# Storing the last block's results in token order over the partitions, by two engines

## The chip, the cores and the metric

One NeuronCore of a Trainium2 chip runs the whole kernel. The metric is the device time of one execution in microseconds, the median over several runs. A profile of one execution stands beside it; its span runs from the first to the last instruction.

## The reference

A causal depthwise convolution over seven tokens, whose weights are the softmax of a small table (one row per head of 24 channels), is followed by a two-layer network with an exact Gelu:

```python
w = softmax(weight, axis=-1)                      # [8 heads, 7 taps]
x_pad = zeros of 6 tokens before each sequence, then x    # x: [8, 4096, 192]
out = einsum('hk,bskhg->bshg', w, windows_of_7(x_pad))    # depthwise convolution
x = out.reshape(32768, 192)
h = x @ w_in                                      # w_in: [192, 2048]
g = 0.5 * h * (1.0 + erf(h / sqrt(2)))
return g @ w_out                                  # w_out: [2048, 192], f32 result
```

## The kernel before, in words

The 32768 tokens are taken as two halves (`HALF` = 16384) that are worked on together. Each half is cut into `NB` = 33 blocks: six of 256 tokens and 27 of 512 (`WS`). Block n covers tokens `OFF[n]` onwards of both halves. There is no planner; every engine has its own program, written out by hand, and semaphores tie them together.

For each block, DMAs on SP load the input (`load`, L258), VectorE transposes it in squares of 32x32 (L478) and convolves it by multiply-and-add (L501, L508) into `xc`; the first two blocks are convolved by TensorE instead. TensorE then computes the first layer one slice of 128 hidden features at a time (`mm1`, L683): both halves of the tokens stand in one of two PSUM buffers `hp[u % 2]`, 2 x 512 columns. ScalarE applies Gelu to each slice (L612) and writes bf16 into `gT[n % 2]`, in which a slice takes 1024 columns. `mm1` of slice u waits for the Gelu of slice u - 2 through `S_GELU`, since it reuses its buffer. Between the slices of block n, TensorE does the second layer of block n - 1.

Because of the 32x32 transposes and of the way in which the input is loaded, column 32b + r of a block stands for token 16r + b of it. For the Gelu of the last block (n = 32) the slice is read as two halves of four runs of 128 columns and written in runs of 128.

The second layer has two forms. Blocks 6 to 31 (`M0` to `M1` - 1) use `mm2_t` (L747), whose result comes out with channels on the partitions, and VectorE transposes it into `osb` (`evac_t`, L247). The last block, and the first six, use `mm2` (L714): the activations are the weights that are loaded into TensorE, 128 tokens at a time, and the result has tokens on the partitions and the 192 channels in the free dimension. A group g of the last block is 128 tokens of the first half of all tokens and 128 of the second, in two PSUM banks of `ob`; there are four groups. Nothing but this is left for TensorE once the last slice's `mm1` and block 31's `mm2_t` are done. Its order is: groups 0 and 1 in two phases of 16 steps each, the phases alternating between the groups, then groups 2 and 3 in the same manner. Group 0's first eight steps wait for half of the Gelus of the block, its next eight for all of them. Group 1 waits for block 31's last VectorE transpose, and groups 2 and 3 wait in `wait_banks` until the banks that they reuse have been copied.

Each group's result leaves PSUM by `evac` (L227 on ScalarE in the first six blocks, L229 on VectorE in the last): one copy of 2 x 192 columns into `osb`. Partition 32q + k of it holds the token 16k + 4g + q of the block, one of each half. `store_group` (L272) therefore stores it in four DMAs, one for each q: 32 partitions by two halves by 768 bytes, in rows 16 tokens apart. For the last block, q = 0 and 1 go out on SP's queue, 2 and 3 on ScalarE's. `OUTS` counts what each parity of blocks adds to `S_OUT`, and at the end SP waits for all of it.

Of the kernel before, what the change touches and what calls it, by code (L numbers as in the profile page):

```python
# [6 lines left out]
AF = mybir.ActivationFunctionType  # L7
# [4 lines left out]
def bass_lightweight_conv__then__act_gelu_exact_kernel(  # L12
# [10 lines left out]
    F2, C = moe_w_out.shape  # L23
# [4 lines left out]
    HALF = NTOK // 2  # L28
    TB = 512
# [7 lines left out]
    NB = len(WS)  # L37
    OFF = [sum(WS[:n]) for n in range(NB)]
    assert sum(WS) == HALF
    NP = D // 64  # L40
    NF = F // 128
# [17 lines left out]
    outt = out.tensor  # L59
# [5 lines left out]
    NG = [w // 128 for w in WS]  # L65
# [5 lines left out]
    PHC, MMC, EVC = [0], [0], [0]  # L71
# [11 lines left out]
    PLAIN = [NCH[n] > 1 or n == NB - 1 for n in range(NB)]  # L83
    assert all(WS[n] == TB for n in range(M0, NB))

    OUTS = []
    for n in range(NB):
        OUTS.append((64 * NG[n] if PLAIN[n] else 64) + (OUTS[n - 2] if n >= 2 else 0))

    es = ExitStack()  # L90

    def sbt(name, shape, dt):
        return es.enter_context(nc.sbuf_tensor(name, shape, dt))

    def pst(name, shape):
        return es.enter_context(nc.psum_tensor(name, shape, F32))

    def sem(name):
        return es.enter_context(nc.semaphore(name))

    def ap(t, off, pat):
        return bass.AP(t, off, pat)

    with es:
# [20 lines left out]
        gT = [sbt("gT%d" % i, [128, NF * 2 * TB], BF16) for i in range(2)]  # L125
        osb = [sbt("osb%d" % i, [128, 8 * C], F32) for i in range(2)]
        hp = [pst("hp%d" % i, [128, 2 * TB]) for i in range(2)]
# [10 lines left out]
        S_OUT = [sem("S_OUT%d" % i) for i in range(2)]  # L138
# [15 lines left out]
        S_GELU = sem("S_GELU")  # L154
        S_MM2 = sem("S_MM2")
        S_PH = sem("S_PH")
        S_EV = sem("S_EV")
        S_EVA = sem("S_EVA")

        block = es.enter_context(nc.Block())  # L160

        def bank(b, r=slice(0, 128), w=512):
            return ob[r, 512 * (b % 4) : 512 * (b % 4) + w]
# [30 lines left out]
        def banks(m, g):  # L194

            if m < M0:
                return (0, 1) if (G0[m] + g) % 2 == 0 else (2, 3)
            r = NP * (M1 - 1 - M0)
            e = (G0[m] - G0[M1] + g) % 2
            return sorted((b % 4 for b in ((r + 3, r), (r + 1, r + 2))[e]))  # L200

        def wait_ev(e, m, g):

            if m < NA:
                e.wait_ge(S_EVA, G0[m] + g + 1)
            else:
                e.wait_ge(S_EV, EVC[m] + g + 1)

        def wait_banks(t, m, g):

            k = G0[m] + g
            if m < M0:
                if k >= 2:
                    t.wait_ge(S_EVA, k - 1)
            else:
                e = k - G0[M1]
                t.wait_ge(S_EV, EVC[M1] + (-2 if e == 0 else e - 1))

        def evac(e, m, g):
            e.wait_ge(S_MM2, MMC[m] + g + 1)  # L220
            if m >= 2 and g == 0:
                e.wait_ge(S_OUT[m % 2], OUTS[m - 2])
            b0, b1 = banks(m, g)
            dst = ap(osb[m % 2], g * C, [[8 * C, 128], [4 * C, 2], [1, C]])
            src = ap(ob, 512 * b0, [[2048, 128], [512 * (b1 - b0), 2], [1, C]])
            if m < NA:
                e.activation(out=dst, in_=src, func=AF.Copy).then_inc(S_EVA)  # L227
            else:
                e.tensor_copy(dst, src).then_inc(S_EV)  # L229

# [34 lines left out]
        def store_group(e, m, g, qs=(0, 1, 2, 3)):  # L267

            mb = WS[m] // 32
            wait_ev(e, m, g)  # L270
            for q in qs:
                e.dma_start(  # L272
                    ap(
                        outt,
                        (OFF[m] + 4 * g + q) * C,
                        [[mb * C, 32], [HALF * C, 2], [1, C]],
                    ),
                    ap(
                        osb[m % 2],
                        32 * q * 8 * C + g * C,  # L280
                        [[8 * C, 32], [4 * C, 2], [1, C]],
                    ),
                ).then_inc(S_OUT[m % 2], 16)
# [109 lines left out]
        def _(v):  # L393
# [142 lines left out]
            side = [((2, (0, 3, 5)[p]), conv_out, 1, p) for p in range(NP)]  # L536
# [2 lines left out]
                    side.append((at, evac_t, v, n, j))  # L539
            for n in range(M1, NB):  # L540
                for g in range(NG[n]):
                    side.append(((n + 3, g), evac, v, n, g))
            side.sort(key=lambda q: q[0])
            for b in range(2, NB):
                if b in PC:
# [9 lines left out]
        @block.scalar  # L555
        def _(a):
            a.wait_ge(S_WARM, 1)
            a.activation(out=hot[:, 0:1], in_=warm[0:1, 0:1], func=AF.Exp).then_inc(S_ACTP)
            load(a, 0, (2, 3))
            a.wait_ge(S_ACTP, 1)  # L560
            a.wait_ge(S_PRO, 1)
            a.activation(
                out=wex[:, :],
                in_=wsb[:, :],
                func=AF.Exp,
                bias=wmx[:, 0:1],
                accum_out=wsm[:, 0:1],
            ).then_inc(S_ACTP)
            a.activation(out=hot[:, 1:2], in_=warm[0:1, 0:1], func=AF.Gelu).then_inc(S_HOT)
            for p in range(NP):  # L570
                a.wait_ge(S_TR, p + 1)
                a.activation(  # L572
                    out=ap(xTb[0], p * XB + HL, [[NP * XB, 128], [1, WS[0]]]),
                    in_=ap(xT[0], p * XW + HL, [[NP * XW, 128], [1, WS[0]]]),
                    func=AF.Copy,
                ).then_inc(S_CAST[0])
            for p in range(NP):
                a.wait_ge(S_PC, p + 1)
                a.activation(  # L579
                    out=xc[0][:, p * TB : p * TB + WS[0]],  # L580
                    in_=bank(CONVB[0][p], w=WS[0]),
                    func=AF.Copy,
                ).then_inc(S_PCE)

            due = {(1, 6): [(0, 0)]}
            for m in range(NA):
                if m >= 1:
                    due[m + 1, NSL[m + 1] // 2] = [(m, 0)]
                due[m + 2, 0] = [(m, 1)]
            for n in range(NB):  # L590
                w = WS[n]
                for i in range(NSL[n]):
                    u = SL0[n] + i
                    c = NCH[n]
                    for k in due.get((n, i), []):
                        evac(a, *k)
                    a.wait_ge(S_MM1, u + 1)
                    if i == 0 and n >= 2:
                        a.wait_ge(S_MM2, MMC[n - 1])
                    if M0 <= n < M1:  # L600

                        src = [[2 * TB, 128], [1, 2 * TB]]
                        dst = [[NF * 2 * TB, 128], [1, 2 * TB]]
                    elif not PLAIN[n]:

                        src = [[2 * TB, 128], [w // 4, 8], [32, w // 128], [1, 32]]
                        dst = [[NF * 2 * TB, 128], [32, 8], [256, w // 128], [1, 32]]
                    else:

                        src = [[2 * TB, 128], [TB, 2], [128, 4], [1, 128]]  # L610
                        dst = [[NF * 2 * TB, 128], [128, 2], [256, 4], [1, 128]]
                    a.activation(  # L612
                        out=ap(gT[n % 2], i * c * 2 * w, dst),
                        in_=ap(hp[u % 2], 0, src),
                        func=AF.Gelu,
                    ).then_inc(S_GELU)

            for g in range(NG[NB - 1]):
                store_group(a, NB - 1, g, (2, 3))

        @block.tensor
        def _(t):
# [70 lines left out]
            def mm2(m, g, ph, i):  # L693
# [4 lines left out]
                if i == 0:  # L698
                    if ph == 0:
                        wait_banks(t, m, g)  # L700
                    else:
                        t.wait_ge(S_PH, PHC[m] + g + 1)
# [25 lines left out]
            def mm2_t(m, ps, i):  # L728

                w = WS[m]  # L730
                if i == 0:
                    if ps < 2:
                        if m == M0:
                            t.wait_ge(S_EVA, G0[M0] - 1 + ps)
                        else:
# [57 lines left out]
        @block.sync  # L793
        def _(sp):
            sp.dma_start(wsb[:, :], ap(wt, 0, [[KS, H], [1, KS]])).then_inc(S_WSB, 16)  # L795
            load(sp, 0, (0, 1))
            sp.wait_ge(S_WIN[0], 32)
            load(sp, 1, (0, 1))
            sp.wait_ge(S_XG[3], 64)
            for n in range(1, NB):  # L800
                if n + 3 < NB:
                    load(sp, n + 3)
                store(sp, n - 1)
            for g in range(NG[NB - 1]):
                store_group(sp, NB - 1, g, (0, 1))
            for s in range(2):
                sp.wait_ge(S_OUT[s], OUTS[NB - 1 if (NB - 1) % 2 == s else NB - 2])

# [27 lines left out]
```

## Time and profile before

| what | value |
|---|---|
| median of 3 runs | 686.33 us (686.32 to 689.21) |
| the profiled execution's own time | 686.27 us |
| its span | 684.5 us |
| TensorE busy | 677.3 us (99% of the span), clock 1.000 |
| VectorE busy | 580.5 us (85%) |
| ScalarE busy | 532.6 us (78%) |
| Gelu instructions (L612) | 512 of 128x1024, 1024 ns each |
| copies of the last block (L229) | 4 of 128x384, 557 ns each |
| stores of the last block (L272) | 16 DMAs of 48 KB, 8 on SP and 8 on ScalarE's queue |
| last TensorE work ends | 681.05 us |

A line of a group gives the source line, the engine and operation, the tile written and the tile read, the shape and the count; then its busy time and the mean length of one instruction; then the idle time of the engine just before them and what ended it. In the timeline a line gives start, length, engine and line, and the idle time before it in brackets; several instructions in a row are merged. PEld is the loading of weights into TensorE, which runs beside its matmuls.

### The profile page before, as it was taken

To read this page: it belongs to the slowest core of one execution; us is meant where nothing else is said; L and a number is where in the kernel's file an instruction comes from. 1 tells how busy PE (TensorE), PEld (TensorE's weight loads), DVE (VectorE), ACT (ScalarE), POOL (GpSimd) and SP (SyncE) were. 2 spreads that over 40 slices of the span, in tenths; PEclk is the share of its full clock that TensorE was granted. 3 is DMA by queue.
4 is the path that set the end of the run, shared out by engine and by line. 5 is a ranking of instruction groups with operands and counts; after the bars stand their busy time and mean duration, and the time that the engine had idled before them with its cause. 6 is when DMAs were issued, how large, how long until landed. Compare 5 with 4: busy or idle time off the path is not lost.

```text
span 684.5 us, 27314 instructions
## 1 busy us (share of the span) xinstructions
PE 677.3 (99%) x12548; PEld 409.0 (60%) x12548; DVE 580.5 (85%) x914; ACT 532.6 (78%) x536; POOL 46.0 (7%) x97
## 2 busy tenths in 40 slices
PE   8999999999999999999999999999999999999997
PEld 4899655555555555555555555555555555555556
DVE  7999999888899888898888898888898888998702
ACT  6788987877787777787877878777778777877771
POOL 8110000000000000000000000000000000000000
PEclk9999999999999999999999999999999999999999
DMA  8544531344432344422444422444322444221224
GB/s 135 95 107 99 117 61 32 64 94 95 94 67 50 76 94 95 93 52 55 85 94 95 88 51 53 95 94 95 72 54 66 95 94 95 61 53 31 48 49 94
DMA packets 133234, 53.66 MB, mean 78 GB/s; under 512 B 127552, under 2 KB 132960, under 8 KB 133120
## 3 DMA queue, kind: packets, MB, share of 16 engines
q1 hardware_dynamic: 128144, 48.78, 33.3%
q0 software_dynamic: 3792, 2.56, 2.4%
q8 instruction: 98, 1.61, 1.0%
q10 hardware_dynamic: 1184, 0.59, 0.3%
q14 instruction: 16, 0.13, 0.1%
HBM read 28.31 MB, written 25.17 MB: 78 GB/s over the span
## 4 chain that ended last, share of the span: by engine, by line
PE 96%; ACT 2%; DMA 1%; issue 0%; DVE 0%; SPq 0%
PE hp L683 47%; PE ob L747 42%; PE ob L714 6%; ACT gT L612 2%; PE ob L640 1%; DMA xin<-in_x_dram 1%; ACT osb L227 0%; DVE osb L247 0%; SPq L258 0%; DVE osb L229 0%; DVE xT L478 0%; ACT xTb L572 0%; SPq L795 0%; ACT xc L579 0%
## 5 line engine op out<-in xcount | busy, mean ns | idle before, releaser
L612 ACT ACTIVATE gT<-hp 128x1024 bf16<-128x1024 f32 x512 | 523.4, 1024 | 132.7 <-PE hp L683 129.6
L683 PE MATMUL hp<-xc,win 64*64 64x512 bf16 (+2 forms) x6048 | 418.5, 366 | 1.1 <-ACT gT L612 0.7
L747 PE MATMUL ob<-gT,wout 64*64 64x512 bf16 x5376 | 366.3, 376 | 0.0
L508 DVE SCALAR_TENSOR_TENSOR acc<-xT,wcol,acc 128x512 f32<-128x512 f32 (+1 forms) x495 | 314.0, 697 | 0.0
L683 PEld LDWEIGHTS hp<-xc,win 64*64 64x64 bf16 (+1 forms) x6048 | 187.7, 106 | 135.6 <-ACT gT L612 2.1
L747 PEld LDWEIGHTS ob<-gT,wout 64*64 64x64 bf16 x5376 | 172.1, 118 | 123.0
L247 DVE STREAM_TRANSPOSE osb<-ob 128x512 f32<-128x512 f32 x84 | 73.7, 880 | 86.8 <-PE ob L747 86.8
L478 DVE STREAM_TRANSPOSE xT<-xin 128x512 f32<-128x512 f32 (+1 forms) x105 | 78.5, 799 | 0.2 <-DMA xin<-in_x_dram 0.2
L508 DVE SCALAR_TENSOR_TENSOR xc<-xT,wcol,acc 128x512 bf16<-128x512 f32 (+1 forms) x99 | 65.1, 711 | 0.0
L374 POOL COPY xT<-xT 128x558 f32<-128x558 f32 x33 | 21.6, 654 | 578.6 <-DVE xT L478 578.6
L501 DVE TENSOR_SCALAR acc<-xT,wcol 128x512 f32<-128x512 f32 (+1 forms) x99 | 56.1, 618 | 1.1
L714 PE MATMUL ob<-wout,gT 64*128 64x192 bf16 x1024 | 52.2, 243 | 0.3
L714 PEld LDWEIGHTS ob<-wout,gT 64*128 64x128 bf16 x1024 | 43.5, 94 | 6.5 <-PE ob L714 0.6
L357 POOL COPY xT<-xT 128x18 f32<-128x18 f32 x30 | 11.6, 387 | 1.4 <-DVE xc L461 1.4
L229 DVE COPY osb<-ob 128x384 f32<-128x384 f32 x4 | 2.2, 557 | 7.8 <-PE ob L714 7.8
L625 PE MATMUL hp<-warm 128*128 128x512 bf16 x16 | 5.7, 533 | 1.3 <-DVE warm L394 1.3
L640 PE MATMUL ob<-xTb,dg 64*64 64x256 bf16 x84 | 5.3, 271 | 1.1 <-ACT xTb L572 1.1
L227 ACT ACTIVATE osb<-ob 128x384 f32<-128x384 f32 x12 | 5.8, 486 | 0.0
L258 POOL DMA_DIRECT2D xin<-in_x_dram x10 | 5.8, 588 | 0.0
L640 PEld LDWEIGHTS ob<-xTb,dg 64*64 64x64 bf16 x84 | 4.3, 106 | 2.2 <-ACT xTb L572 1.6
L625 PEld LDWEIGHTS hp<-warm 128*128 128x128 bf16 x16 | 2.0, 129 | 4.5 <-issue 2.7
L324 POOL DMA_DIRECT2D win<-in_moe_w_in_dram x6 | 3.9, 651 | 0.0
(32 smaller groups left out, 21.7 us busy)
## 6 DMA issues: line engine op xcount, KB each, us to landing
xin<-in_x_dram SPq DMA_DIRECT2D x116, 192.0 KB, 4.4
out_dram<-osb SPq DMA_DIRECT2D x112, 192.0 KB, 3.6
out_dram<-osb SPq DMA_DIRECT2D x56, 48.0 KB, 1.7
xin<-in_x_dram SPq DMA_DIRECT2D x12, 96.0 KB, 2.7
xin<-in_x_dram POOLq DMA_DIRECT2D x10, 96.0 KB, 2.7
wout<-in_moe_w_out_dram POOLq DMA_DIRECT2D x1, 768.0 KB, 8.6
win<-in_moe_w_in_dram POOLq DMA_DIRECT2D x4, 96.0 KB, 4.2
win<-in_moe_w_in_dram POOLq DMA_DIRECT2D x2, 192.0 KB, 5.3
```

What stands on the lines that cost most here:

```text
L247: v.transpose(ap(osb[m % 2], j, [[8 * C, 128], [C // 2, TB // 32], [NP, 32]]), bank(ring(m, j)),).then_inc(S_EV)
L357: g.tensor_copy(dst, ap(xT[(n - 1) % 2], WS[n - 1] + 31, [[NP * XW, 128], [XW, NP], [32, HB]],),).then_inc(S_HALO)
L374: g.tensor_copy(ap(t, 1, [[NP * tw, 128], [tw, NP], [32, HB], [1, 31]]), ap(t, WS[n], [[NP * tw, 128], [tw, NP], [32, HB], [1, 31]]),).the ...
L478: v.transpose(ap(xT[n % 2], p * XW + HL, [[NP * XW, 128], [1, w]]), ap(xin[n % NX], p, [[TB // 32 * DQ, 128], [DQ, w // 32], [NP, 32]],),) ...
L501: ins = v.tensor_scalar(a, src, wk, None, ALU.mult)
L508: ins = v.scalar_tensor_tensor(dst, src, wk, a, op0=ALU.mult, op1=ALU.add)
L612: a.activation(out=ap(gT[n % 2], i * c * 2 * w, dst), in_=ap(hp[u % 2], 0, src), func=AF.Gelu,).then_inc(S_GELU)
L625: t.matmul(hp[1][:, 0:512], warm[:, 0:128], warm[:, :])
L640: ins = t.matmul(bank(CONVB[n][p], r, w), dg[r, d0 : d0 + 64], xTb[PC[n]][r, x0 : x0 + w], start=(k == KS - 1), stop=(k == 0), tile_positi ...
L683: ins = t.matmul(hp[u % 2][fo : fo + fw, o : o + w], win[r, f1 : f1 + fw], xc[n % 2][r, p * TB : p * TB + w], start=(p == 0), stop=(p == N ...
L714: ins = t.matmul(bank(bb[sub], w=C), gT[m % 2][r, c0 : c0 + 128], wout[r, CH[i] * C : (CH[i] + 1) * C], start=(ph == 0 and i == 0), stop=( ...
L747: ins = t.matmul(bank(ring(m, j), slice(64 * h, 64 * h + 64), w), ap(wout, 64 * hf * NF * C + CH[i] * C + j, [[NF * C, 64], [NP, 64]],), g ...
```

## The change

Only the last block is touched. Its Gelu becomes two instructions of 512 elements for each slice, one for each half of the tokens, and writes the results into `gT` in token order: of the 128 columns of a group, column 16k + b gets the token of that number. TensorE, which loads these columns as weights, then puts the group's tokens on the partitions in order. A group's two halves leave PSUM separately: VectorE copies the first half's 192 columns (`evac_half` with h = 0, counted in `S_EV`), ScalarE the second half's (h = 1, counted in the new semaphore `S_EVB`). `store_half` stores each half as one DMA of 128 partitions by 768 bytes, which is one contiguous stretch of the output: the first half on SP's queue, the second on ScalarE's. `wait_banks` waits for both copies for groups 2 and 3. `OUTS` counts eight DMAs for the last block, where it counted sixteen.

```diff
-        OUTS.append((64 * NG[n] if PLAIN[n] else 64) + (OUTS[n - 2] if n >= 2 else 0))
+        k = 32 * NG[n] if n == NB - 1 else 64 * NG[n] if PLAIN[n] else 64
+        OUTS.append(k + (OUTS[n - 2] if n >= 2 else 0))
...
+        S_EVB = sem("S_EVB")
...
                 e = k - G0[M1]
                 t.wait_ge(S_EV, EVC[M1] + (-2 if e == 0 else e - 1))
+                if e >= 2:
+                    t.wait_ge(S_EVB, e - 1)
...
+        def evac_half(e, g, h):
+
+            m = NB - 1
+            e.wait_ge(S_MM2, MMC[m] + g + 1)
+            if g == 0:
+                e.wait_ge(S_OUT[m % 2], OUTS[m - 2])
+            dst = osb[m % 2][:, (4 * h + g) * C : (4 * h + g + 1) * C]
+            src = bank(banks(m, g)[h], w=C)
+            if h == 0:
+                e.tensor_copy(dst, src).then_inc(S_EV)
+            else:
+                e.activation(out=dst, in_=src, func=AF.Copy).then_inc(S_EVB)
+
+        def store_half(e, g, h):
+
+            m = NB - 1
+            if h == 0:
+                wait_ev(e, m, g)
+            else:
+                e.wait_ge(S_EVB, g + 1)
+            e.dma_start(
+                ap(outt, (h * HALF + OFF[m] + 128 * g) * C, [[C, 128], [1, C]]),
+                osb[m % 2][:, (4 * h + g) * C : (4 * h + g + 1) * C],
+            ).then_inc(S_OUT[m % 2], 16)
...
-                    side.append(((n + 3, g), evac, v, n, g))
+                    side.append(((n + 3, g), evac_half, v, g, 0))
...
+                    if n == NB - 1:
+
+                        for h in range(2):
+                            ins = a.activation(
+                                out=ap(
+                                    gT[n % 2],
+                                    i * 2 * w + 128 * h,
+                                    [[NF * 2 * TB, 128], [1, 16], [256, 4], [16, 8]],
+                                ),
+                                in_=ap(
+                                    hp[u % 2],
+                                    TB * h,
+                                    [[2 * TB, 128], [32, 16], [8, 4], [1, 8]],
+                                ),
+                                func=AF.Gelu,
+                            )
+                        ins.then_inc(S_GELU)
+                        continue
...
             for g in range(NG[NB - 1]):
-                store_group(a, NB - 1, g, (2, 3))
+                evac_half(a, g, 1)
+                store_half(a, g, 1)
...
             for g in range(NG[NB - 1]):
-                store_group(sp, NB - 1, g, (0, 1))
+                store_half(sp, g, 0)
```

## The prediction

> **What bounds the kernel now.** I read the chain of waits first, then the cost groups, then the last 40 us in order of time, because only the last block (n = 32) is edited. The page's chain and groups:
>
> ```profile
> PE 96%; ACT 2%; DMA 1%; issue 0%; DVE 0%; SPq 0%
> ...
> L612 ACT ACTIVATE gT<-hp 128x1024 bf16<-128x1024 f32 x512 | 523.4, 1024 | 132.7 <-PE hp L683 129.6
> L683 PE MATMUL hp<-xc,win 64*64 64x512 bf16 (+2 forms) x6048 | 418.5, 366 | 1.1 <-ACT gT L612 0.7
> ...
> L229 DVE COPY osb<-ob 128x384 f32<-128x384 f32 x4 | 2.2, 557 | 7.8 <-PE ob L714 7.8
> ...
> L227 ACT ACTIVATE osb<-ob 128x384 f32<-128x384 f32 x12 | 5.8, 486 | 0.0
> ```
>
> TensorE is the chain. ScalarE's Gelu (L612) waits for TensorE 129.6 us in all and TensorE almost never for it. How thin that cover is, the timeline of the last block shows (start, length, what ran, idle before):
>
> ```profile
> 649.05 0.82 PE L683 MATMUL hp<-xc,win 64*64 64x512 bf16 x12
> ...
> 664.60 1.02 ACT L612 ACTIVATE gT<-hp 128x1024 bf16<-128x1024 f32 x1 [0.27 <-PE hp L683]
> 665.89 1.02 ACT L612 ACTIVATE gT<-hp 128x1024 bf16<-128x1024 f32 x1 [0.27 <-PE hp L683]
> 667.19 1.02 ACT L612 ACTIVATE gT<-hp 128x1024 bf16<-128x1024 f32 x1 [0.27 <-PE hp L683]
> 668.48 2.10 ACT L612 ACTIVATE gT<-hp 128x1024 bf16<-128x1024 f32 x2 [0.27 <-PE hp L683]
> ```
>
> Starts are 1.295 us apart (1.51 three times, 1.08 at the end): TensorE's pace of a slice. ScalarE works 1.02 of it and idles 0.27. The stretch from 649.9 to 670.6 us holds the 16 Gelus of the last block, the first at 649.92, straight after L683 ended. Then the end, in the timeline and in the waits from 668 us on:
>
> ```profile
> 669.99 1.57 DVE L247 STREAM_TRANSPOSE osb<-ob 128x512 f32<-128x512 f32 x2 [6.45 <-PE ob L747]
> 670.64 0.61 PEld L714 LDWEIGHTS ob<-wout,gT 64*128 64x128 bf16 x16 [0.16 <-ACT gT L612]
> 671.62 9.19 PEld L714 LDWEIGHTS ob<-wout,gT 64*128 64x128 bf16 x224 [0.37 <-DVE osb L247]
> ...
> 675.07 7.46 ACTq L272 DMA_DIRECT2D out_dram<-osb  x8
> 675.16 7.29 SPq L272 DMA_DIRECT2D out_dram<-osb  x8
> ...
> 681.08 0.56 DVE L229 COPY osb<-ob 128x384 f32<-128x384 f32 x1 [0.76 <-PE ob L714]
> ```
> ```profile
> PEld ob L714 <- DVE osb L247: 0.4, 1, 0.4
> PEld ob L714 <- ACT gT L612: 0.2, 1, 0.2
> ```
>
> TensorE takes the second half of group 0's first phase at 670.64, released by the last Gelu (ended 670.58), then waits 0.37 us for block 31's transposes, then runs 9.43 us to 681.05. One VectorE copy and the last stores follow, to 684.5: 3.45 us behind TensorE.
>
> [...] The trace gives the same slope, (1024 - 384)/(1024 - 256) = 0.833 ns from L612 and L579 (128x256, 384 ns), but a fixed 171 ns; five Gelus in a row took 4.92 us, so the overlap is (5 x 1.024 - 4.92)/4 = 50 ns. [...]
>
> **The change part by part.**
>
> *Gelu split and permuted.* Sixteen instructions of 1024 elements become 32 of 512. They still read PSUM in order, but write each 2-byte result 32 bytes from the one before (step 16 bf16); before, runs of 128 were contiguous. If the stride is free, one takes 171 + 512 x 0.833 = 598 ns, and in a row 548 ns: a pair 1.10 us, inside 1.295, so hidden by TensorE's slice. The last pair then ends about 0.15 us later than 670.58, and the 0.37 us wait for L247 takes that.
> If the stride costs, ScalarE becomes the bound, as hp has two buffers and L683 of slice u+2 waits for Gelu u. With a pair of P us back to back, the last Gelu ends at 649.92 + 16P + 0.05, TensorE resumes 0.06 later, and the delay against 671.62 - 0.61 = 671.01 is **16P - 20.98 us**: nothing up to P = 1.31.
> The price is unknown, so I bound it. Below: 0.833 ns an element, P = 1.10; a gain is excluded, as the count of elements and the fixed parts don't fall. Above: three cycles an element, P = 2 x (0.121 + 512 x 0.0025) = 2.80, delay 23.8. For nothing: VectorE's transpose L247 writes 4-byte results 12 bytes apart at 880 ns, and L478, which writes contiguously, takes 862. [...] For a price: POOL's memset of 128x18 with 128-byte steps takes 133 ns against 99 for 128x1, 2.0 ns an element, and in bf16 with 64-byte steps 179 against 102, 4.5 ns (POOL spans are rough). I take **two cycles**[...]: 121 + 512 x 1.667 = 974 ns, P = 1.95, delay 16 x 1.95 - 20.98 = **+10.2 us**. The transposes are not late next: they follow block 31's last L747, which is released by the Gelu two slices earlier, at about 678.4, and end by 680.1, before TensorE resumes at 681.3.
>
> *Evacuation.* Four VectorE copies of 384 (557 ns) become four of 192 plus four ScalarE copies of 192. VectorE: 557 - 192 x 1.04 = 357 ns (its conv row rises 255 ns for 256 elements; bounds 279, half, to 557). ScalarE: 171 + 160 = 331 ns, side by side with VectorE. Only group 3 is on the path: -0.20 us; the others hide under L714. ScalarE is free there, its Gelus done.
>
> *Stores.* Sixteen DMAs of 48 KB become eight of 96 KB: one each on SP and ACT per group. An issue took a median of 432 ns on SP and 452 on ACT, and the second of a queue started some 0.35 us after the first; that goes. Data per group is the same. Landing: 48 KB took 1.6 us at the fastest and 2.0 in the median, 192 KB 3.9; I take 2.0 for 96 KB (bounds 1.6 and 3.0). After: copies end 681.44, issued 681.47, landed 683.45, where SP's last wait now ends at 684.1: **-0.65 us** with the 0.20 (range -1.0 to +0.4).
>
> *Queues and waits.* ScalarE's copy of group g+1 stands behind its DMA issue of group g. Groups 2 and 3 finish 1.32 us apart; 0.33 + 0.05 + 0.45 fits, and even the longest ACT issue, 0.79, gives 1.17. TensorE's added wait on S_EVB for groups 2 and 3 asks for copies that have 1.32 us of cover, a phase of another group: group 0's banks are copied while group 1's second phase runs, group 1's while group 2's first phase runs; behind it stand L714's weight loads, all waiting together. The S_OUT wait asks for stores of block 30, long landed. I cost these at nothing; the covers gone, 0.1 us each. SP and ACT each have one issue fewer per group; POOL and the input loads are untouched (last load issued at 598 us).
>
> *Sum.* +10.2 - 0.65 = +9.6 us on the profiled execution's 686.27 (span 684.5 and 1.8 around it), which stands 0.06 under the median 686.33: **695.9 us**.
>
> **The rivals.**
> 1. *The stride is free.* For: [...]the rows here show no penalty for 12 bytes. [...] Then only the end moves: 686.33 - 0.65 = 685.7 us, not slower. It decides at P = 1.31, that is (1.31/2 - 0.121)/512 = 1.04 ns an element.
> 2. *A partial price,* 1.25 ns an element: P = 1.52, delay 3.4, net +2.7: 689.1 us.
> 3. *Three cycles:* +23.8 - 0.65: 709.5 us. Only the rough bf16 POOL row speaks for it.
> 4. *The larger DMA takes back what the shorter queue gives:* 3.0 us to landing with a free stride, end at 684.5 against 684.1: 686.7 us. Against: the same bytes go to the same queues.
> 5. *The change doesn't do what it says,* the ACT store lagging behind SP's: at most a second issue, 0.45 us: 686.1.
>
> **How the numbers follow.** A measurement of this kernel can tell about 0.5% (3.4 us) from no change. Two cycles, or near it: 0.56; three: 0.06; partial: 0.06; free, with 4 and 5: 0.32. Of the partial case most is within 0.5%, and 0.02 is kept for a gain over 3.4 us, for which the 3.45 us tail leaves hardly room. Faster 0.02, same 0.36, slower 0.62. The likeliest case's own range: 1.8 to 2.2 cycles, P from 1.78 to 2.12, gives +6.8 to +12.3 net: 693 to 698.6 us. The whole range reaches down to the free case: 685.4 to 698.6; three cycles are left out.
>
> **What would show it.** Gelu instructions of about 1.02 us for 512 elements, back to back with no idle from 650 us on; L683 in the last block waiting for ScalarE; TensorE's last resume near 681 us. If they last 0.60 us with idle left between pairs, the stride is free and my forecast is wrong. For the end: copies of 0.36 and 0.33 us, one issue per queue and group, under 3 us from TensorE's end to the span's.

## The result and the profile after

The changed kernel took **736.88 us** (median of 4 runs, 735.48 to 738.75) against 686.33 us before: a ratio of 1.0728, 95% interval 1.069 to 1.0767, so it is slower by 7.3%. The direction and the mechanism were forecast, the size was not: 695.9 us, with a range that ended at 698.6. The profiled execution took 737.45 us, with a span of 735.1 us.

The page of the changed kernel, first the chain by engine, then the groups that answer to those shown of before:

```profile
PE 87%; ACT 11%; DMA 1%; issue 0%; SPq 0%; DVE 0%
...
L731 PE MATMUL hp<-xc,win 64*64 64x512 bf16 (+2 forms) x6048 | 423.7, 370 | 31.2 <-ACT gT L644 30.1
...
L644 ACT ACTIVATE gT<-hp 128x512 bf16<-128x512 f32 x32 | 69.7, 2681 | 0.1
...
L244 DVE COPY osb<-ob 128x192 f32<-128x192 f32 x4 | 1.4, 358 | 16.0 <-PE ob L762 16.0
...
L246 ACT ACTIVATE osb<-ob 128x192 f32<-128x192 f32 x4 | 1.3, 331 | 11.5 <-PE ob L762 11.5
```

ScalarE's share of the chain went from 2% to 11%. The 32 Gelus of the last block (L644) occupy 69.7 us without idle time; before, the 16 of that block took 16.4 us. One lasts 2681 ns from its start to its end, but neighbours overlap: 32 of them fit in 69.67 us, so the mean distance from start to start is (69.67 - 2.68)/31 = 2.16 us. TensorE's first layer, which before waited for Gelu 0.7 us in all, now waits 30.1 us.

The two copies at the end last 358 and 331 ns, as forecast (357 and 331). With the 557 ns of before, VectorE's shows (557 - 358)/192 = 1.04 ns an element, the slope that the forecast had used.

The timeline of the last block and the end (start, length, idle before):

```profile
650.13 69.67 ACT L644 ACTIVATE gT<-hp 128x512 bf16<-128x512 f32 x32
...
719.85 7.32 PE L762 MATMUL ob<-wout,gT 64*128 64x192 bf16 x118 [5.13 <-ACT gT L644]
725.65 0.33 ACT L246 ACTIVATE osb<-ob 128x192 f32<-128x192 f32 x1 [5.85 <-PE ob L762]
...
732.25 0.33 ACT L246 ACTIVATE osb<-ob 128x192 f32<-128x192 f32 x1 [0.99 <-PE ob L762]
```

The last Gelu ends at 719.80, and TensorE, which had waited 5.13 us for it, resumes at 719.85. Stretches of that time show a second loss. The columns are stretch, its length, then busy time and count for TensorE, weight loads, VectorE, ScalarE and GpSimd, then the granted TensorE clock, the DMA share and GB/s. The changed kernel, then the kernel before:

```profile
714.80:717.70 2.90, 0.00 (x0) 0.00 (x0) 0.38 (x1) 2.90 (x3) 0.00 (x0) 1.00 0.38 74
717.80:719.80 2.00, 0.00 (x0) 0.00 (x0) 0.00 (x0) 2.00 (x1) 0.00 (x0) 0.50 0.92 205
719.80:722.00 2.20, 2.15 (x28) 2.06 (x30) 0.00 (x0) 0.00 (x0) 0.00 (x0) 0.50 0.32 73
722.00:725.70 3.70, 3.70 (x64) 3.59 (x62) 0.05 (x1) 0.05 (x1) 0.00 (x0) 0.65 0.00 0
725.70:732.30 6.60, 6.51 (x158) 6.28 (x154) 1.07 (x4) 0.99 (x4) 0.00 (x0) 1.00 0.22 68
```
```profile
671.00:674.50 3.50, 3.35 (x82) 3.13 (x78) 0.59 (x2) 0.00 (x0) 0.00 (x0) 1.00 0.43 84
674.50:681.10 6.60, 6.54 (x160) 6.31 (x154) 1.67 (x4) 0.00 (x0) 0.00 (x0) 1.00 0.61 139
```

From resuming to the end of group 0 TensorE took 725.62 - 719.85 = 5.77 us; before, the same work without the waits took 674.45 - 671.01 = 3.44. (671.01 is where the work would have begun without the wait for the transposes, as in the prediction; 725.62 and 674.45 are just before the first copies start.) The granted clock had fallen to 0.50 during the wait, and over 722.00 to 725.70 it was 0.65 on average. The other three groups took 6.60 us in both. The spans therefore add up: the block began 0.21 us later, TensorE's resumption was delayed by a further 719.85 - 671.22 = 48.63, the lower clock added 2.33, and the end shrank from 3.45 to 735.1 - 732.22 = 2.88. The sum is 0.21 + 48.63 + 2.33 - 0.57 = 50.6 us, which is 735.1 - 684.5.

### The profile page after: what moved, and what is told of

Read it like the earlier page. It is cut to its first block, busy times and chain, and to the rows that moved or that the text cites. A ratio compares the mean times of both kernels' runs of the same rounds, so it can differ in the third digit from the quotient of the medians.

```text
span 735.1 us, 27329 instructions
## 1 busy us (share of the span) xinstructions
PE 692.6 (94%) x12548; PEld 412.1 (56%) x12548; DVE 579.5 (79%) x914; ACT 586.7 (80%) x556; POOL 45.8 (6%) x97
## 4 chain that ended last, share of the span: by engine, by line
PE 87%; ACT 11%; DMA 1%; issue 0%; SPq 0%; DVE 0%
PE hp L731 43%; PE ob L795 38%; ACT gT L644 9%; PE ob L762 6%; ACT gT L659 2%; DMA xin<-in_x_dram 1%; PE ob L688 1%; ACT osb L231 0%; SPq L287 0%; DVE xT L507 0%; ACT xTb L601 0%; SPq L843 0%; ACT xc L608 0%; DVE osb L244 0%
## 5 line engine op out<-in xcount | busy, mean ns | idle before, releaser
L659 ACT ACTIVATE gT<-hp 128x1024 bf16<-128x1024 f32 x496 | 506.5, 1023 | 128.9 <-PE hp L731 125.8
L731 PE MATMUL hp<-xc,win 64*64 64x512 bf16 (+2 forms) x6048 | 423.7, 370 | 31.2 <-ACT gT L644 30.1
L795 PE MATMUL ob<-gT,wout 64*64 64x512 bf16 x5376 | 372.4, 381 | 0.0
L644 ACT ACTIVATE gT<-hp 128x512 bf16<-128x512 f32 x32 | 69.7, 2681 | 0.1
L762 PE MATMUL ob<-wout,gT 64*128 64x192 bf16 x1024 | 54.8, 251 | 5.3 <-ACT gT L644 5.1
L762 PEld LDWEIGHTS ob<-wout,gT 64*128 64x128 bf16 x1024 | 46.1, 98 | 11.9 <-ACT gT L644 5.4
```

What stands on the lines that cost most here:

```text
L644: ins = a.activation(out=ap(gT[n % 2], i * 2 * w + 128 * h, [[NF * 2 * TB, 128], [1, 16], [256, 4], [16, 8]],), in_=ap(hp[u % 2], TB * h, ...
L659: a.activation(out=ap(gT[n % 2], i * c * 2 * w, dst), in_=ap(hp[u % 2], 0, src), func=AF.Gelu,).then_inc(S_GELU)
L731: ins = t.matmul(hp[u % 2][fo : fo + fw, o : o + w], win[r, f1 : f1 + fw], xc[n % 2][r, p * TB : p * TB + w], start=(p == 0), stop=(p == N ...
L762: ins = t.matmul(bank(bb[sub], w=C), gT[m % 2][r, c0 : c0 + 128], wout[r, CH[i] * C : (CH[i] + 1) * C], start=(ph == 0 and i == 0), stop=( ...
L795: ins = t.matmul(bank(ring(m, j), slice(64 * h, 64 * h + 64), w), ap(wout, 64 * hf * NF * C + CH[i] * C + j, [[NF * C, 64], [NP, 64]],), g ...
```

## Experiments

Ratios compare each kernel with runs of the kernel before on the same chip. Those had a median of 686.44 us beside experiments 1 to 4, 686.45 beside 5, 6, keep_busy and moving_strided, and 687.39 beside keep_busy_end, conv_order and 9.

**1. The Gelu alone (gelu_only).** The kernel before, with this in its Gelu loop:

```diff
+                    if n == NB - 1:
+                        for h in range(2):
+                            ins = a.activation(out=ap(gT[n % 2], i * 2 * w + 128 * h,
+                                    [[NF * 2 * TB, 128], [1, 16], [256, 4], [16, 8]]),
+                                in_=ap(hp[u % 2], TB * h, [[2 * TB, 128], [32, 16], [8, 4], [1, 8]]),
+                                func=AF.Gelu)
+                        ins.then_inc(S_GELU)
+                        continue
```

> Only the change's two Gelu instructions for each slice; copies and stores of the last block as before (the rows of its result then go to other places, so the output's last block is in another order). Theory (the scattered Gelu is all of the loss): 736.88 + 0.6 = about 737.5 us, 32 Gelus at 2.18 us apart, the granted clock again below 1 in the last block. Rival (the new copies, stores or waits cost some of it): clearly under 736.

It took 736.97 us, ratio 1.0736 (1.0716 to 1.0755), with TensorE's first layer waiting 31.3 us for Gelu:

```profile
L701 PE MATMUL hp<-xc,win 64*64 64x512 bf16 (+2 forms) x6048 | 423.0, 369 | 32.4 <-ACT gT L615 31.3
```

The loss lies in the Gelu; the new copies, stores and waits cost none of it that can be seen. With two runs the 0.5 us of the end can't be told.

**2. The end alone (tail_only).** The changed kernel without the lines above.

> The changed kernel with the Gelu of before (one instruction, contiguous runs); each half of a group is copied by its own engine and stored as one DMA, but in the old order of the rows, so the output's last block is in another order. Theory (the end gets shorter by what the profile of the changed kernel shows there, 2.88 us from TensorE's end to the span's end against 3.45): 686.33 - 0.6 = 685.7 us. Rival (the end gives nothing): 686.3 us.

It took 685.91 us, ratio 0.9993 (0.9985 to 1.0002). The interval includes no change, so the gain isn't shown by the times alone, but their difference of 0.53 us agrees with the forecast of 0.65 and with the 0.57 in the trace of the changed kernel. In this kernel's own timeline the copies of the last group start at 681.33, so TensorE ended near 681.30, and the span ends at 684.1: 2.8 us.

**3. The split alone (split_contiguous).** The kernel before with two Gelus for each slice, in the old runs of 128:

```diff
-                                    [[NF * 2 * TB, 128], [1, 16], [256, 4], [16, 8]],
+                                    [[NF * 2 * TB, 128], [256, 4], [1, 128]],
...
-                                    [[2 * TB, 128], [32, 16], [8, 4], [1, 8]],
+                                    [[2 * TB, 128], [128, 4], [1, 128]],
```

> The kernel before with each Gelu of the last block in two instructions of 512 elements, both written in the contiguous runs of 128 of before. Theory (splitting is free): 32 instructions of 0.598 us, pairs of 1.10 to 1.15 us inside TensorE's slice of 1.295 us, 686.3 us, same as before within 0.2. Rival (two instructions for each slice make ScalarE the bound): the idle time before a pair goes to zero and the time rises by a microsecond or more.

It took 686.4 us, ratio 1.0 (0.9992 to 1.0009). Its timeline of ScalarE shows pairs that fit:

```profile
668.46 1.08 ACT L615 ACTIVATE gT<-hp 128x512 bf16<-128x512 f32 x2 [0.21 <-PE hp L701]
```

A pair lasts 1.08 us and 0.21 us of idle time is left. Splitting is free, so the loss lies in the permuted write. Whether its steps or its short inner loops are the reason is left to the next two experiments.

**4. The price by step (scan).** Each slice of the last block has its own step, on the writing side (slices 0 to 7) or the reading side (8 to 15):

```diff
+        SCAN = [1, 2, 4, 8, 16, 32, 64, 256, 1, 2, 4, 8, 16, 32, 128, 512]
...
+                        plain = [[1, 2 * TB]]
+                        moved = [[1, s], [s, 2 * TB // s]] if s > 1 else plain
```

> The kernel before, in whose last block each of the 16 Gelus (one instruction of 1024 elements each, ScalarE) has a step of its own: slices 0 to 7 read in order and write with steps of 1, 2, 4, 8, 16, 32, 64, 256 bf16 elements (2 to 512 bytes) in the inner loop; slices 8 to 15 write in order and read PSUM with steps of 1, 2, 4, 8, 16, 32, 128, 512 f32. Behind the last store ScalarE and VectorE each copy 512 elements eight times from an SBUF tile to spare tiles: f32 with steps of 2, 4, 8, 16 elements (VectorE 1, 4, 8, 16), then bf16 with steps of 1, 4, 8, 16. The last block's values stand in another order, so it computes something else there; the lengths of the single instructions are what is read. Theory (the price is ScalarE's scattered 2-byte write, per element): the write of step 16 takes about 4.5 to 5.2 us for 1024 elements, as 32 bytes apart or more, steps of 1 and 2 about 1.02 us, and every read about 1.02 us. Rival 1 (short inner loops cost, not the step): the changed kernel's inner loop is 8 long; here step 16 has a loop of 64 and would take near 1.02 us, and steps of 64 and 256 (loops of 16 and 4) far more, reads with the same loops likewise. Rival 2 (any access to a new line costs, reads too): reads with steps from 4 elements on rise as the writes do. The spare copies tell whether f32 writes pay as bf16 ones do (if the 2-byte size is the reason, f32 at 32 bytes stays near 0.60 us) and whether VectorE pays (if the memory is the reason, it does).

The run took 711.02 us in all. The timeline of ScalarE, one line for each instruction (start, length): Gelus that write with steps of 1, 2, 4, 8, 16, 32, 64 and 256 elements, then Gelus that read with steps of 1 to 8:

```profile
650.18 1.02 ACT L628 ACTIVATE gT<-hp 128x1024 bf16<-128x1024 f32 x1
651.48 1.33 ACT L628 ACTIVATE gT<-hp 128x1024 bf16<-128x1024 f32 x1 [0.27 <-PE hp L720]
652.77 2.46 ACT L628 ACTIVATE gT<-hp 128x1024 bf16<-128x1024 f32 x1
654.98 4.81 ACT L628 ACTIVATE gT<-hp 128x1024 bf16<-128x1024 f32 x1
659.29 4.88 ACT L628 ACTIVATE gT<-hp 128x1024 bf16<-128x1024 f32 x1
663.71 4.92 ACT L628 ACTIVATE gT<-hp 128x1024 bf16<-128x1024 f32 x1
668.15 5.05 ACT L628 ACTIVATE gT<-hp 128x1024 bf16<-128x1024 f32 x1
672.71 5.05 ACT L628 ACTIVATE gT<-hp 128x1024 bf16<-128x1024 f32 x1
677.27 1.34 ACT L628 ACTIVATE gT<-hp 128x1024 bf16<-128x1024 f32 x1
678.70 1.02 ACT L628 ACTIVATE gT<-hp 128x1024 bf16<-128x1024 f32 x1
680.22 1.02 ACT L628 ACTIVATE gT<-hp 128x1024 bf16<-128x1024 f32 x1 [0.49 <-PE hp L720]
681.51 1.02 ACT L628 ACTIVATE gT<-hp 128x1024 bf16<-128x1024 f32 x1 [0.27 <-PE hp L720]
```

The price rises up to a step of 8 elements, 16 bytes, and is nearly flat from there (4.31 to 4.56 us from start to start). From start to start, a write of step 8 takes 659.29 - 654.98 = 4.31 us for 1024 results, 4.2 ns each; step 4, with two results in each 16 bytes, takes 2.21 us, again about 4.3 ns for every 16 bytes touched. So at these two steps the price goes by the stretch of 16 bytes, which is what a new line in the expectations means here, and not by the result. The theory had given a step of two elements as free; it costs 0.3 us more (1.33 against 1.02). Reads of PSUM took 1.02 us at steps of 2, 4 and 8 elements, as writes in order do (the read of step 1, at 1.34, starts before the slow one ahead of it has ended); those of 16 and 32 took 1.02 as well, and those of 128 and 512 together 2.10, as a pair in order did before. Short inner loops are refuted by step 16, whose loop of 64 costs nearly as much as step 256 with a loop of 4 (4.44 and 4.56 us).

The spare copies of 512 elements from SBUF, in the timeline: ScalarE in f32 with steps of 8, 16 and 32 bytes, then in bf16 with 16 and 32 bytes; then VectorE in bf16 with 2, 8, 16 and 32 bytes:

```profile
699.48 0.68 ACT L652 ACTIVATE scf<-acc 128x512 f32<-128x512 f32 x1 [11.98 <-DVE osb L233]
700.05 1.12 ACT L652 ACTIVATE scf<-acc 128x512 f32<-128x512 f32 x1
700.96 1.16 ACT L652 ACTIVATE scf<-acc 128x512 f32<-128x512 f32 x1
...
704.40 2.51 ACT L652 ACTIVATE scb<-acc 128x512 bf16<-128x512 f32 x1
706.42 2.63 ACT L652 ACTIVATE scb<-acc 128x512 bf16<-128x512 f32 x1
```
```profile
700.16 0.40 DVE L560 CAST sdb<-acc 128x512 bf16<-128x512 f32 x1
700.49 0.72 DVE L560 CAST sdb<-acc 128x512 bf16<-128x512 f32 x1
701.01 1.36 DVE L560 CAST sdb<-acc 128x512 bf16<-128x512 f32 x1
701.97 1.50 DVE L560 CAST sdb<-acc 128x512 bf16<-128x512 f32 x1
```

From start to start, ScalarE's f32 results cost 0.91 us per 512 at 16 bytes, 1.8 ns each, and its bf16 results 2.02 us, 3.9 ns. So both expected reasons hold in part: f32 pays too, and 2-byte results pay about twice as much. VectorE pays as well, 0.96 us per 512 bf16 (701.97 - 701.01), 1.9 ns each. ScalarE's f32 copies ran at the same time as VectorE's, so a mutual delay in these prices is not ruled out; its bf16 copies of 16 and 32 bytes ran alone.

**5. The loops turned round (read_strided).** The whole changed kernel, but the step is put on the reading side:

```diff
-                                    [[NF * 2 * TB, 128], [1, 16], [256, 4], [16, 8]],
+                                    [[NF * 2 * TB, 128], [256, 4], [16, 8], [1, 16]],
...
-                                    [[2 * TB, 128], [32, 16], [8, 4], [1, 8]],
+                                    [[2 * TB, 128], [8, 4], [1, 8], [32, 16]],
```

> The changed kernel, whole, with the two loops of each Gelu turned round: it now reads PSUM with steps (32 columns apart) and writes its 512 results in order, in runs of 128. Theory (the price lies in the write to a new line each time; the step scan showed PSUM reads at 1.02 us for 1024 elements at every step): 0.60 us an instruction, pairs of 1.08 to 1.15 us hidden in the slice, and only the shorter end is left: 685.9 us, as with the end alone. Rival (a permutation in four loops costs whichever side it is on): the same 2.2 us an instruction as in the changed kernel, near 737 us.

It took 685.88 us, ratio 0.9993 (0.9983 to 1.0004). Its group of Gelus in the last block:

```profile
L644 ACT ACTIVATE gT<-hp 128x512 bf16<-128x512 f32 x32 | 17.4, 594 | 3.4 <-PE hp L731 3.4
```

The same permutation of the same results by the same engine takes 594 ns in place of 2681. The rival falls: it is the side of the permutation that decides.

**6. One of two instructions (one_half).** As in 5, for h = 1 only.

> The changed kernel with the loops turned round for the second half of the tokens only: one instruction of each pair still writes 32 bytes apart. By the prediction's own formula with measured occupancies, P = 2.18 + 0.55 = 2.73 us and the delay is 16 x 2.73 - 20.98 = 22.7 us, less 0.5 for the end, plus up to 2 for TensorE's lower clock: 708.5 to 710.6 us. Rival (a fixed cost of switching the pattern, or of the pair, not of each scattered element): nearer to 737 or to 686.

It took 710.09 us, ratio 1.0343 (1.0325 to 1.0361). The Gelus and TensorE's last resumption:

```profile
L644 ACT ACTIVATE gT<-hp 128x512 bf16<-128x512 f32 x32 | 42.7, 1693 | 0.1
```
```profile
693.29 12.88 PE L762 MATMUL ob<-wout,gT 64*128 64x192 bf16 x240 [3.26 <-ACT gT L644]
```

TensorE resumed at 693.29, 22.3 us after 671.01; the block itself began 0.60 us later (650.52 against 649.92), so the Gelus account for 21.7 us. The formula gave 22.7 with the P = 2.73 that was expected, and gives 21.7 with the measured 42.7/16 = 2.67. The formula holds; it had been given a wrong P.

**7. TensorE kept busy (keep_busy, keep_busy_end).** The changed kernel with idle time filled, first ahead of the slices:

```diff
+                    if n == NB - 1 and i >= 2:
+                        if i == 2:
+                            t.wait_ge(S_EV, EVC[M1 - 1])
+                        for _ in range(11):
+                            t.matmul(bank(ring(M1, 0)), warm[:, 0:128], warm[:, :])
```

> The changed kernel with 11 more matmuls of 512 columns ahead of each slice of the last block from the third on, into a PSUM bank that nothing else uses then: 11 x 0.213 = 2.3 us of work in the 2.7 us for which TensorE waits for ScalarE there. Theory (the granted clock falls because TensorE idles; the first group of the end ran at 0.50 and 0.65 and took 5.8 us from the last Gelu's end where it took 3.85): the clock stays near 1, the first group takes 3.9 us, and the time falls by 1.5 to 2 us to about 735. Rival (the clock falls for another reason, with time or with ScalarE's work): no change or slower, 737 us or more.

It took 737.53 us, ratio 1.0743 (1.0724 to 1.0761): no gain, where about 735 was expected. The 11 matmuls took 2.55 us, where 2.3 was expected. The clock over the block (650 to 720 us) rose from 0.72 to 0.98, but TensorE still stood empty for 6.6 us in the last wait. So that wait was filled as well, in `mm2` ahead of step 8 of group 0:

```diff
+                if m == NB - 1 and g == 0 and ph == 0 and i == 8:
+                    for _ in range(40):
+                        t.matmul(ob[:, 512 * (ring(M1, 0) % 4) + C : 512 * (ring(M1, 0) % 4) + 512],
+                                 warm[:, 0:128], warm[:, C:512], start=False, stop=False)
```

> The kernel with 11 more matmuls ahead of each slice of the last block, and in addition 40 matmuls of 320 columns (about 5.3 us) in the last wait for ScalarE, ahead of the second eight steps of group 0, into columns that nothing reads. That last wait stood empty for 6.6 us in the run with the 11 matmuls alone, where the clock was 0.98 up to it and 0.50 after it. Theory (the granted clock falls within microseconds of TensorE's own idling): the clock after the wait is near 1, group 0 is done some 3.9 us after the last Gelu instead of 5.7, and the time is 735 to 735.7 us. Rival (it falls for another reason): 0.50 again after the wait, and 737 us.

It took 734.62 us, ratio 1.0694 (1.0669 to 1.072), a little under what was expected. Stretches after the last wait, first of the run with the slices filled alone, then of this one:

```profile
720.30:722.00 1.70, 1.67 (x22) 1.57 (x24) 0.00 (x0) 0.00 (x0) 0.00 (x0) 0.50 0.00 0
```
```profile
720.00:722.00 2.00, 2.00 (x50) 2.00 (x52) 0.00 (x0) 0.00 (x0) 0.00 (x0) 1.00 0.00 0
```

The 40 matmuls took 5.61 us, and TensorE stood empty for 1.06 us in place of 6.6. The clock is 1.00, group 0 is done 723.47 - 719.92 = 3.55 us after the last Gelu (725.62 - 719.80 = 5.82 in the changed kernel), and the span is 732.9 us, 2.2 less than the changed kernel's 735.1 though more is done. The lower clock came from TensorE's own idling, and it was the last wait that mattered.

**8. Two other places for the permutation.** In moving_strided, TensorE reads `xc` with steps and the Gelu is that of before:

```diff
-                                    xc[n % 2][r, p * TB : p * TB + w],
+                                    ap(xc[n % 2], 64 * hf * NP * TB + p * TB,
+                                        [[NP * TB, 64], [1, 32], [32, 16]]) if n == NB - 1
+                                    else xc[n % 2][r, p * TB : p * TB + w],
```

> Another place for the same permutation: the Gelu is that of before (one instruction of 1024, runs of 128), and in the last block TensorE's first layer reads its moving operand xc with steps of 64 bytes, so that its columns come out in token order; the end is the changed one. It computes the reference. Theory (only ScalarE's writes were the price, and TensorE's reads keep their 0.216 us a step of two to four matmuls): 685.9 us. Rival (TensorE's reads from a new line each time cost as the writes of ScalarE do): the 12 matmuls of a slice take 0.65 us now; at twice that, 16 slices lose 10 us, 696 us.

It took 717.0 us, ratio 1.0443 (1.0428 to 1.0458). My expectation failed, and the rival's 696 was too low as well. TensorE's group in the last block:

```profile
L713 PE MATMUL hp<-xc,win 64*64 64x512 bf16 x192 | 47.5, 1049 | 0.0
```

One matmul lasts 1049 ns, where the line of before in the prediction has 366. Before, a slice's 12 matmuls took 0.65 us of the chain, half of the 1.295. The whole loss, (717.0 - 685.9)/16, is 1.94 us a slice, so they now take about 2.6. In conv_order, VectorE writes `xc` in token order in the last step of the convolution:

```diff
                         dst = xc[n % 2][:, p * TB : p * TB + w]
+                        if n == NB - 1:
+                            dst = ap(xc[n % 2], p * TB, [[NP * TB, 128], [1, 16], [16, 32]])
+                            src = ap(xT[n % 2], p * XW + 32 * kt, [[NP * XW, 128], [32, 16], [1, 32]])
+                            a = ap(acc, p * TB, [[NP * TB, 128], [32, 16], [1, 32]])
```

> A third place for the permutation: VectorE's last step of the last block's convolution (three instructions) writes xc in token order, 2-byte results 32 bytes apart; the Gelu is that of before, the end is the changed one. It computes the reference. In the step scan VectorE's copies of 512 elements to such steps followed each other at 0.96 us. Theory (VectorE pays too, but three times only, and it was done at 646.8 us, 2.2 us before TensorE first read the tile): instructions of about 1.3 to 1.5 us instead of 0.74, up to 1.5 us later, still in time, 685.9 us. Rival (the delay is not covered): 686.5 us or more, with a wait of L731's first slice for VectorE.

It took 688.93 us, ratio 1.0029 (1.0017 to 1.0041). The rival was right, as the timeline shows:

```profile
644.65 6.85 DVE L547 SCALAR_TENSOR_TENSOR xc<-xT,wcol,acc 128x512 bf16<-128x512 f32 x3
...
651.64 0.84 PE L723 MATMUL hp<-xc,win 64*64 64x512 bf16 x12 [2.41 <-DVE xc L547]
```

The three instructions took 6.85/3 = 2.3 us each, more than the copies of experiment 4 led me to expect; why is open. VectorE ended at 651.5, and TensorE waited 2.41 us.

**9. One instruction with the loops turned round (read_strided_one).** As in 5, with one Gelu of 1024 elements that reads `[TB, 2], [8, 4], [1, 8], [32, 16]` and writes `[128, 2], [256, 4], [1, 128]`.

> The kernel with the loops turned round, with one Gelu instruction of 1024 elements for each slice (four loops on the side that reads) in place of two of 512. Theory (ScalarE isn't the bound once it writes in order): 1.02 us an instruction and 685.9 us, the same as with two. Rival (two instructions cost something in the last block): lower than with two by up to 0.2 us.

It took 686.29 us, ratio 0.9984 (0.9972 to 0.9996), with Gelus of 1.02 us. This interval lies just under 1 where that of 5 includes it, but the difference is in the runs of the kernel before (687.39 and 686.45), not in these two kernels (686.29 and 685.88), so whether one instruction is better than two can't be told. Either is a version to keep: no slower than the kernel before, and some 50 us faster than the change as written.

## Why the prediction was wrong

- **The mechanism was right.** Scattered writes made ScalarE the bound, with no idle time from 650 us on. The formula 16P - 20.98 gives 48.7 us with the measured P = 69.67/16 = 4.354; the trace has 48.6. That is mostly bookkeeping, since the measured length of all Gelus goes in; the test of the formula is experiment 6, where it was 1.0 us off with a P taken from other runs.
- **The step that failed is the price of the write,** in "The change part by part": I took two cycles, twice the measured 0.833 ns: 1.667 ns an element, and 974 ns an instruction. That factor was an estimate, and no row of before showed it. Measured, it is 2161 ns from start to start, and with the same fixed 121 ns (2161 - 121)/512 = 4.0 ns. That term accounts for 48.7 - 10.2 = 38.5 of the 41 us that were missed.
- **The upper bound was wrong as well.** I capped it at three times 0.833 ns, 2.5 ns, for which I had no row, and left even that out of the range. The one row of before with 2-byte results far apart, GpSimd's memset in steps of 64 bytes with 4.5 ns an element, stood in my text, and I set it aside as rough. On ScalarE it would have given P = 2 x (121 + 512 x 4.5) ns = 4.85 us, a delay of 56.6 us: near the 48.6, and the range would have held the result. Experiment 4 has the rows that were missing: on ScalarE in bf16, 1024 results took 4.31 us in steps of 16 bytes and 2.21 us in steps of 8, and one instruction in steps of 4 lasted 1.33 us in place of 1.02.
- **The second term that I did not have is TensorE's clock,** +2.33 us. The clock stood at 0.50 from 717.80 us on, 3.1 us into the wait of 5.13; it was 0.50 after a wait of 3.26 us in experiment 6; and it averaged 0.71 from 650 to 714 us, a stretch in which no wait was longer than 2.83 us. It was back at 1.00 from 724.6 us, 4.7 us after TensorE resumed: the mean of 0.65 over 722.00 to 725.70 is 0.50 up to there and 1.00 after it. My own figures (the last L747 released at about 678.4, TensorE resuming at 681.3) implied a wait before the last steps, and I did not ask what it does to the clock.
- **The rest held.** Copies of 357 and 331 ns: 358 and 331. The end: -0.65 forecast, -0.57 in the trace. The new waits and queues cost nothing that can be seen: groups 1 to 3 end at the same distances as before. Splitting the Gelu cost nothing (experiment 3; pairs of 1.08 us, 1.10 forecast), and a free stride would have given 685.7: with the step on the reading side it is 685.9. One reading was off without effect: in the last block of before, starts 1.51 us apart occur twice, not three times.

## What to carry to other kernels

Where a permutation has to ride along with an instruction, put the step on the side that was measured to be free: here ScalarE's Gelu of 512 elements took 594 ns when it read PSUM with the steps, no more than in order (a pair of 1.08 us in experiments 3 and 5), and 2681 ns, one every 2161, when it wrote with them. The free writes here were runs of 128 results, 256 bytes; shorter runs without a price were not shown. Reading with steps is not free everywhere: on TensorE it cost 31 us (experiment 8). If no row shows the price of an access pattern, bound it by the worst row that resembles it, not by a round factor. And when an engine becomes the bound and TensorE starts to wait for microseconds, add what TensorE's clock loses after the wait (2.33 us here, after 5.13 us of waiting).

## What the runs showed of the hardware that I had not expected

- ScalarE's writes in steps of 16 to 512 bytes took 4.2 to 4.45 ns a result in bf16 (1024 results, experiment 4), and in steps of 16 bytes 1.8 ns in f32; VectorE's in steps of 16 bytes took 1.9 ns in bf16.
- ScalarE's reads of PSUM with steps of 8 to 128 bytes took the 1.02 us of reads in order, and those of 512 and 2048 bytes together the 2.10 us of a pair in order (experiment 4).
- TensorE's moving operand read with steps of 64 bytes made a slice of 12 matmuls some four times as long (0.65 to about 2.6 us, experiment 8).
- Two slow ScalarE instructions in a row overlap by 0.52 us (2681 ns long, 2161 apart), where fast ones overlap by 0.05 (in the prediction) to 0.1 (two of 594 ns in 1.08 us, experiment 5), so the mean length of one overstates its cost.
